# Long convolution and spectral mixing: the second and third transforms on 64x64 quadrants of the array, the filter's spectrum stored once, one tick at a time

## The chip, the core and the metric

The kernel runs on one core of one Trainium2 chip. The metric is the device time of one execution in microseconds (us). A core has a matrix engine (TensorE, PE in the profile; its weight loads are a row of their own, PEld), a vector engine (VectorE, DVE), a scalar engine (ScalarE, ACT), GpSimd (POOL) and SyncE (SP); the last two mostly issue DMAs here. Matmul results land in PSUM, which has eight banks of 512 fp32 columns on 128 partitions; everything else lies in SBUF, also on 128 partitions.

## What is computed

`x` is (8, 5696, 128), `h` is (5696, 128). First a long convolution along the sequence, by FFT of the doubled length; then a spectral layer on its result:

```python
L = 2 * S                                    # S = 5696
y = irfft(rfft(x, L, axis=1) * rfft(h, L, axis=0), L)[:, :S]
X = rfft(y, axis=1)                          # over S
Y[:, :64] = X[:, :64] mixed with w_r, w_i    # complex 128x128 per mode, 64 modes
u = y + irfft(Y, S)
out = u + relu(u @ w_ch)                     # (8, 5696, 128) float32
```

## The kernel before

The transform of length 2S is cut into 64 positions `p` and 89 blocks `q`, which gives `NK` = 90 classes `k` of frequencies. Everything is done by matmul in fp16. Three transforms follow each other.

- **First transform** (`a_tile`, and the loop above it for the filter): over `q`, with the constants in `f1_sb`. The two batches of a pair lie on the two halves of the partitions of `a_sb`, each with its 64 positions.
- **Second transform** (`second` for x, `filter_tick` for h): over the 64 positions, for each class `k`. For batch b the contraction runs over the 64 partitions of that batch, and the result has 128 partitions: 64 real parts over 64 imaginary parts. So a matmul has 64 rows and 128 columns of weights (from `m_sb`) and 128 moving columns. Two of them (real and imaginary input) add up in one PSUM region; batch 0 and batch 1 use the two halves of the rows and two banks.
- **Product** (`products`): spectrum of x times spectrum of h. Since the real part needs Xr·Hr and Xi·Hi on different partitions, the kernel holds the filter twice in `h_sb`: as it is, and with its halves swapped by DMAs (`Hs<-Hs`). VectorE makes both products in one instruction of 2048 elements per partition into `u_s`.
- **Third transform** (`third`): back from 64 frequencies to 64 positions, with two constant 128x128 weights `W1` and `W2` for the two products: for each batch two matmuls of 512 columns into one bank. ScalarE copies the bank to `z_s` (call it Z), a DMA on SP writes `z_s` to a scratch tensor in DRAM.
- **Modes** (`modes_of`): the 64 modes of the second layer, summed straight from `z_s` with the constants `g_sb` into bank 7, eight matmuls of 128 rows by 128 columns per tick.

A **tick** is four classes. A group is a pair of batches; there are four groups, and each has 23 ticks (`NT`; the last has two classes). The order of the work is written out by hand in `tick` and kept by every engine's own queue; `Recorder` only puts in the semaphore waits that the data need. For tick t: the second transform of t, its product, the third transform of t−2 (`LC`), the modes of t−3 (`LM`). Before the change odd ticks are twins: after the product of an odd tick t the second transform of t+1 follows at once, so that the second transforms come in blocks of two ticks (32 matmuls).

PSUM in this stage: two slots of two banks for the second transform (`XSLOT`, banks 0 to 3), three banks that rotate for the third (`ZBANK`, 4, 5, 6), bank 7 for the modes. In three of four ticks ScalarE first copies the spectrum from its slot to SBUF (`copied`, into one of two buffers `x_s`), and VectorE multiplies from there; in the fourth (`straight`, t mod 4 = 3) VectorE reads PSUM itself and holds the slot for as long.

Between the ticks of two groups lies the first transform of the next pair (32 `a_tile`, with the last two third transforms of the group among the first of them). Before the first group lies the filter's transform: 32 `a_tile` of group 0 with the 23 `filter_tick` among them. After the last group the transform back over `q`, the mixing, the residual and the output follow (from about 255 us on); the change doesn't touch them.

The two places that the prediction leans on, besides the diff:

```python
    LC, LM = 2, 3
    XSLOT = [0, 2]
    ZBANK = [4, 5, 6]
...
            zb = [turns("z", ZBANK) for b in range(2)]
```

Of the kernel before, what the change touches and what calls it, by code (L numbers as in the profile page):

```python
# [4 lines left out]
P = 128  # L5
# [118 lines left out]
def bass_long_conv_fft__then__afno_spectral_mix_kernel(nc, x, h, moe_w_r, moe_w_i, moe_w_ch, out):  # L124
# [66 lines left out]
    c_f1 = const("cF1", f1)  # L191
    c_w = const("cW", np.concatenate([w1, w2, np.eye(P)], axis=1))
    c_s4 = const("cS4", s4t)
# [30 lines left out]
    a_h = take(2 * HW * 2)  # L224
    h_sb = at("Hs", 2 * HW, F16, a_h)
    a_g = take(HW * 2)
# [28 lines left out]
    ZP = ZB * 2 * D  # L255
    a_h2, a_xt = a_h + HW * 2, a_x + 4 * S + 2 * B * P
    a_as1, a_m2 = a_as + 2 * S, a_m + 4 * S
# [34 lines left out]
    R = Recorder(nc)  # L292
    for name, n in (("c", 16), ("x", 26), ("z", 8), ("w", 16), ("t", 10), ("s", 8), ("o", 12), ("p", 16), ("q", 10)):
        R.ring(name, n)
# [98 lines left out]

    W1, W2, WI = wc_sb[:, 0:P], wc_sb[:, P:2 * P], wi_sb[:, :]
    XSLOT = [0, 2]
# [58 lines left out]

    HEND = [1, 5, 11, 17, NT - 1]

    def filter_tick(t, banks, eng):
        n = len(ticks[t])
        hb = banks
        for i, k in enumerate(ticks[t]):  # L460
            for r in range(2):
                for dh in range(2):
                    mm(pv(hb[dh], i * DH, [[1, DH]]),
                       ap(m_sb, MW, J * dh, J, k * 3 * J + (J if r == 0 else 0) + dh * J, [[1, P]]),
                       ap(ah_sb, HW, J * dh, J, (2 * k + r) * DH, [[1, DH]]), r == 0, r == 1,
                       AHT + mtok(k) + [("ag", k)], [bank(hb[dh])])
        lo, hi = KT * t * D, (KT * t + n) * D
        old = once("xr", [t_ for r_ in XR for t_ in r_]) if t == 0 else []
        evac(h_sb[:, lo:hi], pv(hb[0], 0, [[DH, n], [512, 2], [1, DH]]), [bank(hb[0]), bank(hb[1])], [("h", t, 0)],
             eng=eng, after=old)  # L470
        if t in HEND:
            g0 = ([-1] + HEND)[HEND.index(t)] + 1
            lo = KT * g0 * D
            for p0, p1 in ((0, J), (J, 0)):
                dma("sync", h_sb[p0:p0 + J, HW + lo:HW + hi], h_sb[p1:p1 + J, lo:hi], "s", [("h", i, 0) for i in range(g0, t + 1)],
                    [("h", i, 1, p0) for i in range(g0, t + 1)])

# [9 lines left out]

    H_ALL = [("h", t, 0) for t in range(NT)] + [("h", t, 1, p0) for t in range(NT) for p0 in (0, J)]
    U_ALL = [("u", i) for i in range(NU)] + [("xs", i) for i in range(NXS)] + \
# [60 lines left out]

    onchip = {}

    def copied(g_, t, sl):
        n = len(ticks[t])
        e = onchip[(g_, t)] = turns("e", list(range(NXS)))
        evac(bass.AP(x_s[e], 0, [[1024, P], [512, 2], [1, n * D]]), pv(sl, 0, [[512, 2], [1, n * D]]), [bank(sl), bank(sl + 1)],
             [("xs", e)], eng="scalar")
        return e

    def twin(g_, t):  # L560
        return t % 2 == 1

# [3 lines left out]
    def slot_of(g_, t):  # L566
        if t == 0:
            return XSLOT[0]
        return XSLOT[((t - 1) // 4 + t) % 2]

    def second(g_, t):
        sl = slot_of(g_, t)
        for i, k in enumerate(ticks[t]):
            for r in range(2):
                for b in range(2):
                    col = k * 3 * J + (J if r == 0 else 0) + b * J
                    mm(pv(sl + b, i * D, [[1, D]]),
                       ap(m_sb, MW, J * b, J, col, [[1, P]]),
                       ap(a_sb, AW, J * b, J, (2 * k + r) * D, [[1, D]]), r == 0, r == 1,
                       AST + mtok(k), [bank(sl + b)])  # L580

    def products(g_, t, sl):
        n = len(ticks[t])
        bk = [bank(sl), bank(sl + 1)]
        i = t % NU
        hv = bass.AP(h_sb, KT * t * D, [[2 * HW, P], [HW, 2], [0, 2], [1, n * D]])
        uv = bass.AP(u_s[i], 0, [[2048, P], [1024, 2], [512, 2], [1, n * D]])
        src = pv(sl, 0, [[0, 2], [512, 2], [1, n * D]])
        if t == 0:
            e = turns("e", list(range(NXS)))  # L590
            evac(bass.AP(x_s[e], 512, [[1024, P], [1, n * D]]), pv(sl + 1, 0, [[1, n * D]]), [bank(sl + 1)], [("xs", e)], eng="scalar")
            hv = bass.AP(h_sb, 0, [[2 * HW, P], [HW, 2], [1, n * D]])
            for b, s_, tok, done in ((0, pv(sl, 0, [[0, 2], [1, n * D]]), bank(sl), ("u", i)),
                                     (1, bass.AP(x_s[e], 512, [[1024, P], [0, 2], [1, n * D]]), ("xs", e), ("u0", i))):
                R.add("vector", lambda e, b=b, s_=s_: e.tensor_tensor(bass.AP(u_s[i], b * 512, [[2048, P], [1024, 2], [1, n * D]]), s_, hv, MULT),  # L595
                      [tok, ("h", t, 0), ("h", t, 1, 0), ("h", t, 1, J)], [done])
            return
        if not straight(g_, t):
            e = onchip.get((g_, t))
            if e is None:  # L600
                e = copied(g_, t, sl)
            src, bk = bass.AP(x_s[e], 0, [[1024, P], [0, 2], [512, 2], [1, n * D]]), [("xs", e)]
        R.add("vector", lambda e: e.tensor_tensor(uv, src, hv, MULT),  # L603
              bk + [("h", t, 0), ("h", t, 1, 0), ("h", t, 1, J)], [("u", i)])

# [9 lines left out]
    def third(g_, s_):  # L615
        if 0 <= s_ < NT:
            n = len(ticks[s_])
            i, zi = s_ % NU, zroom(g_, s_)
            zb = [turns("z", ZBANK) for b in range(2)]
            for b in range(2):  # L620
                for r in range(2):
                    mm(pv(zb[b], 0, [[1, n * D]]), (W1, W2)[r], u_s[i][:, r * 1024 + b * 512:r * 1024 + b * 512 + n * D],
                       r == 0, r == 1, [("u", i), ("wc",)] + ([("u0", i)] if s_ == 0 and b else []), [bank(zb[b])])
                evac(bass.AP(z_s[zi], b * D, [[1024, P], [2 * D, n], [1, D]]),
                     pv(zb[b], 0, [[D, n], [1, D]]), [bank(zb[b])], [("zs", zi, b)], eng="scalar",
                     after=once(("zx", zi, b), Z_OLD) if zi >= NZ else ())
            zo = (g_ * NK + KT * s_) * P * 256
            dma("sync", bass.AP(zs, zo, [[256, P], [P * 256, n], [1, 256]]),
                bass.AP(z_s[zi], 0, [[1024, P], [256, n], [1, 256]]), "z",
                [("zs", zi, 0), ("zs", zi, 1)], [("zd", g_, s_)])  # L630

    def modes_of(g_, s_):
        if 0 <= s_ < NT:
            zi = zroom(g_, s_)
            for b in range(2):
                for i, k in sorted(enumerate(ticks[s_]), key=lambda q: (s_ > 0 or q[1] != 1, q)):
                    if k % 2:
                        o, off, n, sl = pv(MB, b * P, [[1, P]]), (k + 1) // 2 * P, P, (k + 1) // 2
# [5 lines left out]
                    mm(o, z_s[zi][:, i * 256 + b * P:i * 256 + b * P + P], g_sb[:, off:off + n],  # L644
                       k == 1 and b == 0, k == NK - 1 and b == 1, [("g", sl // GP), ("zs", zi, b)], [bank(MB)])
# [255 lines left out]
```

## Time and profile before

| | us |
|---|---|
| median of three runs (380.42 to 383.9) | 381.24 |
| the profiled execution's own time | 385.21 |
| its span, first to last instruction | 383.1 |
| PE busy | 362.8 |
| DVE busy | 305.9 |
| ACT busy | 303.7 |
| filter and first transform of group 0 | 28.3 to 51.1 |
| ticks of the four groups begin at | 51.1, 105.6, 160.0, 214.4 |
| the last block of the modes begins; the back transform starts | 254.3; 255.7 |

The profile is of one execution, on one core, whose mean granted TensorE clock was 0.985. "Busy" of PE is the time in which at least one matmul was under way; matmuls overlap, and one of 128 moving columns is shown as some 217 ns long although the next may start 56 ns after it. So occupancy is better read from start to start: when a block of matmuls begins, and when the next block does. The helper that issues matmuls is line 320, copies are line 308 (ACT) and 312 (DVE), scaled copies 310 and 314; groups are told apart by the tiles behind them: `ps<-As,M` is the second transform of x, `ps<-Ah,M` that of the filter, `ps<-U,Wc` the third, `ps<-G,Zs` (or `Zt`) the modes, `ps<-F,Xin` the first transform; `Xs<-ps` is the copy of the spectrum, `U<-Xs,Hs` the product from SBUF and `U<-ps,Hs` that from PSUM, `Zs<-ps` (or `Zt<-ps`) the evacuation of the third transform.

### The profile page before, as it was taken

How to read it: one execution, taken by the hardware profiler on the slowest of the kernel's cores; microseconds unless marked ns; L12 is line 12 of the kernel's file. 1: busy time of each engine (PE TensorE's matmuls, PEld its weight loads, DVE VectorE, ACT ScalarE, POOL GpSimd, SP SyncE). 2: the span in 40 equal slices, each digit the busy share in tenths (PEclk: the TensorE clock that was granted, in tenths of full speed). 3: DMA queues.
4: the chain of work that ended last, by engine and by line, in shares of the span. 5: the costliest groups of instructions: out<-in, count | busy, mean ns of one | idle time of the engine just before them, and what ended most of it. 6: DMA issues, size and time to landing. Idle time of an engine off the chain costs nothing.

```text
span 383.1 us, 12483 instructions
## 1 busy us (share of the span) xinstructions
PE 362.8 (95%) x5372; PEld 283.6 (74%) x5372; DVE 305.9 (80%) x334; ACT 303.7 (79%) x497; POOL 81.5 (21%) x133
## 2 busy tenths in 40 slices
PE   7999989999989999899999899999979999999994
PEld 7988766667856667766668666668868988988873
DVE  6968898998989998889989887854327767777876
ACT  1358889998989998899998899993447676677785
POOL 8400002320832312723303011339000000000000
PEclk9999999999999999999999999996989999999999
DMA  7999689997999996999997199999999999999768
GB/s 147 194 279 346 151 217 224 282 269 231 116 128 250 231 274 147 145 161 242 241 268 104 15 319 360 339 336 382 407 380 373 361 413 412 412 404 372 303 267 351
DMA packets 83985, 103.94 MB, mean 271 GB/s; under 512 B 22062, under 2 KB 68910, under 8 KB 80450
## 3 DMA queue, kind: packets, MB, share of 16 engines
q1 hardware_dynamic: 59643, 67.73, 51.2%
q0 software_dynamic: 24288, 35.43, 44.0%
q8 instruction: 42, 0.69, 0.7%
q14 instruction: 12, 0.10, 0.1%
HBM read 70.61 MB, written 51.12 MB: 318 GB/s over the span
## 4 chain that ended last, share of the span: by engine, by line
PE 65%; DMA 12%; ACT 10%; DVE 5%; POOL 5%; issue 2%; POOLq 0%; DVEq 0%
PE ps L320 65%; ACT As L310 6%; DMA Xr<-in_x_dram 5%; DMA ZT4b<-zscr 4%; DMA zscr<-Zt 3%; DVE As L314 2%; POOL Xr L317 2%; DVE U L595 1%; ACT R L835 1%; ACT UT L308 1%; ACT Zs L308 1%; DVE O L836 1%; POOL ZT1b L508 0%; POOL ZT3b L508 0%; POOLq L105 0%
## 5 line engine op out<-in xcount | busy, mean ns | idle before, releaser
L320 PE MATMUL ps<-U,Wc 128*128 128x512 f16 (+1 forms) x368 | 94.5, 376 | 0.0
L603 DVE TENSOR_TENSOR U<-Xs,Hs 128x2048 f16<-128x2048 f16 (+1 forms) x68 | 80.5, 1187 | 10.7 <-ACT Xs L308 9.6
L308 ACT CAST Xs<-ps 128x1024 f16<-128x1024 f32 (+1 forms) x72 | 69.5, 971 | 7.0 <-PE ps L320 4.8
L836 DVE TENSOR_TENSOR O<-ps,R 128x512 f32<-128x512 f32 x81 | 52.5, 685 | 21.4 <-ACT R L835 13.9
L308 ACT CAST Zs<-ps 128x512 f16<-128x512 f32 (+1 forms) x126 | 66.1, 605 | 0.0
L835 ACT ACTIVATE R<-ps 128x512 f32<-128x512 f32 x96 | 50.9, 573 | 17.7 <-PE ps L320 17.2
L314 DVE TENSOR_SCALAR As<-ps 128x720 f16<-128x720 f32 x64 | 53.6, 880 | 7.7 <-PE ps L320 6.2
L310 ACT ACTIVATE As<-ps 128x720 f16<-128x720 f32 (+1 forms) x68 | 48.9, 771 | 10.4 <-PE ps L320 9.4
L320 PE MATMUL ps<-F,Xin 128*128 128x180 f16 x512 | 53.7, 250 | 3.4 <-DVE Xin L356 0.9
L320 PEld LDWEIGHTS ps<-F,Xin 128*128 128x128 f16 x512 | 45.3, 155 | 10.7 <-DVE As L314 3.1
L320 PE MATMUL ps<-WI,UT 128*128 128x256 f16 x360 | 52.6, 282 | 0.5 <-DVE O L836 0.4
L320 PE MATMUL ps<-As,M 64*128 64x128 f16 x1440 | 48.6, 217 | 4.5 <-DVE U L595 3.5
L320 PEld LDWEIGHTS ps<-U,Wc 128*128 128x128 f16 x368 | 28.2, 97 | 28.8 <-ACT Zs L308 6.8
L320 PEld LDWEIGHTS ps<-As,M 64*128 64x128 f16 x1440 | 40.3, 94 | 10.3 <-DVE U L595 4.1
L317 POOL DMA_DIRECT2D Xt<-in_x_dram x48 | 25.0, 524 | 102.2 <-PE ps L320 101.6
L603 DVE TENSOR_TENSOR U<-ps,Hs 128x2048 f16<-128x2048 f32 x20 | 45.7, 2283 | 0.0
L308 ACT CAST UT<-ps 128x712 f16<-128x712 f32 x40 | 30.0, 752 | 19.2 <-PE ps L320 18.4
L320 PEld LDWEIGHTS ps<-WI,UT 128*128 128x128 f16 x360 | 39.6, 152 | 4.5 <-issue 1.9
L320 PE MATMUL ps<-IBs,C 128*128 128x356 f16 x128 | 40.5, 326 | 0.7
L320 PEld LDWEIGHTS ps<-G,Zs 128*128 128x128 f16 x492 | 27.0, 96 | 12.7 <-DMA G<-cG 0.3
L308 ACT CAST Zt<-ps 128x512 f16<-128x512 f32 (+1 forms) x58 | 30.9, 602 | 0.4 <-DMA zscr<-Zt 0.4
L312 DVE CAST UT<-ps 128x712 f16<-128x712 f32 x24 | 21.3, 890 | 11.7 <-PE ps L320 11.7
(87 smaller groups left out, 513.0 us busy)
## 6 DMA issues: line engine op xcount, KB each, us to landing
out_dram<-O SPq DMA_DIRECT2D x39, 512.0 KB, 8.6
zscr<-Zs SPq DMA_DIRECT2D x60, 256.0 KB, 7.2
Xt<-in_x_dram POOLq DMA_DIRECT2D x24, 320.0 KB, 6.6
zscr<-Zt SPq DMA_DIRECT2D x28, 256.0 KB, 7.0
W<-wscr POOLq DMA_DIRECT2D x4, 1024.0 KB, 8.7
M<-cM POOLq DMA_DIRECT2D x5, 720.0 KB, 20.8
ZT0a<-zscr SPq DMA_DIRECT2D x3, 1024.0 KB, 13.1
Xr<-in_x_dram POOLq DMA_DIRECT2D x8, 320.0 KB, 14.3
```

What stands on the lines that cost most here:

```text
L308: R.add(e, lambda h_: h_.copy(dst, src), reads, writes, after=after)
L310: R.add(e, lambda h_: h_.activation(dst, src, COPY, scale=scale), reads, writes, after=after)
L312: R.add(e, lambda h_: h_.tensor_copy(dst, src), reads, writes, after=after)
L314: R.add(e, lambda h_: h_.tensor_scalar_mul(dst, src, scale), reads, writes, after=after)
L317: R.add(eng, lambda h_: h_.dma_start(dst, src), reads, writes, ring=ring, after=after)
L320: R.add("tensor", lambda h_: h_.matmul(o, l, r, start=st, stop=sp), reads, writes)
L595: R.add("vector", lambda e, b=b, s_=s_: e.tensor_tensor(bass.AP(u_s[i], b * 512, [[2048, P], [1024, 2], [1, n * D]]), s_, hv, MULT), [tok, ...
L603: R.add("vector", lambda e: e.tensor_tensor(uv, src, hv, MULT), bk + [("h", t, 0), ("h", t, 1, 0), ("h", t, 1, J)], [("u", i)])
L835: R.add("scalar", lambda e: e.activation(rv, src_r, RELU), bk, [("r", i % NR)], after=once(("r", i % NR), G_ALL + XTT + [("y", 0), ("y", 1 ...
L836: R.add("vector", lambda e: e.tensor_tensor(ov, src_u, rv, ADD), bk + [("r", i % NR)], [key + (h_,)], after=once(key, old))
```

## The change

- **Second transform.** A matmul now makes either the real or the imaginary part: 64 rows by 64 columns of weights, 128 moving columns. The 64 result partitions are the lower ones for even classes and the upper ones for odd classes; real and imaginary parts lie side by side in the free dimension (`HB` = 256 columns apart). Four matmuls in a row (`QUADS`) go to the four quadrants of the array: (batch, class parity) = (0,0), (1,1), (0,1), (1,0). A tick has 32 of them where it had 16. `filter_tick` is changed in the same way, and the filter then serves both products from one copy: the DMAs that swapped its halves are gone.
- **Product.** The same number of elements (2048 per partition); the access patterns follow the new layout.
- **Third transform.** The rows are now class parity and frequency, so the contraction is over 64 partitions too: 16 matmuls of 64x64 weights with 512 moving columns (both batches) where there were four of 128x128. The four terms (`at_`) run in the outer loop, the quadrants in the inner one; the two banks of a tick belong to the two class parities, and both are evacuated after the last of the 16 matmuls.
- **Order.** No twins: each tick has its second transform, its product, and the third transform of t−2. The slots of the second transform simply alternate. The modes come for four ticks at once, after the third transform, at t = 6, 10, 14, 18 and 22 (32 matmuls of 128x128); the last three ticks' modes come at the group's end as before.

```diff
-    w1 = np.block([[c, s], [-c, -s]])
-    w2 = np.block([[-s, c], [-s, c]])
+    wj = np.concatenate([c, s, -c, -s], axis=1)
...
+    HB = KT // 2 * D
+    HL = 2 * HB * NT
+    h_sb = at("Hs", HL, F16, a_h)
...
+    QUADS = ((0, 0), (1, 1), (0, 1), (1, 0))
+    MOFF = ((J, 0), (2 * J, J))
...
     def filter_tick(t, banks, eng):
...
+        n2 = len(ticks[t]) // 2
+        for i in range(n2):
+            for ri in range(2):
+                for r in range(2):
+                    for dh, c_ in QUADS:
+                        k = KT * t + 2 * i + c_
+                        mm(pv(banks[dh], (2 * ri + i) * DH, [[1, DH]], J * c_, J),
...
-        if t in HEND:
...
-                dma("sync", h_sb[p0:p0 + J, HW + lo:HW + hi], h_sb[p1:p1 + J, lo:hi], "s", [("h", i, 0) for i in range(g0, t + 1)],
...
     def slot_of(g_, t):
-        if t == 0:
-            return XSLOT[0]
-        return XSLOT[((t - 1) // 4 + t) % 2]
+        return XSLOT[t % 2]
 
     def second(g_, t):
         sl = slot_of(g_, t)
-        for i, k in enumerate(ticks[t]):
-            for r in range(2):
-                for b in range(2):
-                    col = k * 3 * J + (J if r == 0 else 0) + b * J
-                    mm(pv(sl + b, i * D, [[1, D]]),
-                       ap(m_sb, MW, J * b, J, col, [[1, P]]),
...
+        for i in range(len(ticks[t]) // 2):
+            for ri in range(2):
+                for r in range(2):
+                    for b, c_ in QUADS:
+                        k = KT * t + 2 * i + c_
+                        mm(pv(sl + b, ri * HB + i * D, [[1, D]], J * c_, J),
+                           ap(m_sb, MW, J * b, J, k * 3 * J + MOFF[ri][r] + b * J, [[1, J]]),
...
     def products(g_, t, sl):
...
+        hv = bass.AP(h_sb, 2 * HB * t, [[HL, P], [HB, 2], [0, 4], [1, n]])
+        uv = bass.AP(u_s[i], 0, [[2048, P], [1024, 2], [HB, 4], [1, n]])
+        src = pv(sl, 0, [[0, 2], [HB, 4], [1, n]])
...
     def third(g_, s_):
...
-            zb = [turns("z", ZBANK) for b in range(2)]
-            for b in range(2):
-                for r in range(2):
-                    mm(pv(zb[b], 0, [[1, n * D]]), (W1, W2)[r], u_s[i][:, r * 1024 + b * 512:r * 1024 + b * 512 + n * D],
...
+            zb = [turns("z", ZBANK) for c_ in range(2)]
+            for at_, (off, w_) in enumerate(((0, (0, 1)), (HB, (3, 0)), (1024, (3, 0)), (1024 + HB, (2, 3)))):
+                for c_, rz in QUADS:
+                    mm(pv(zb[c_], 0, [[1, 2 * n2 * D]], J * rz, J), ap(wc_sb, 2 * P, J * c_, J, w_[rz] * J, [[1, J]]),
+                       ap(u_s[i], 2048, J * c_, J, off, [[512, 2], [1, n2 * D]]),
...
+            for c_ in range(2):
+                evac(bass.AP(z_s[zi], 2 * D * c_, [[1024, P], [D, 2], [4 * D, n2], [1, D]]),
+                     pv(zb[c_], 0, [[n2 * D, 2], [D, n2], [1, D]]), [bank(zb[c_])], [("zs", zi, c_)], eng="scalar",
...
     def tick(g_, t):
...
-            of_two = t > 0 and twin(g_, t - 1)
-            if not of_two:
-                second(g_, t)
+            second(g_, t)
             products(g_, t, slot_of(g_, t))
-            if twin(g_, t):
-                second(g_, t + 1)
-                if straight(g_, t):
-                    copied(g_, t + 1, slot_of(g_, t + 1))
...
         third(g_, t - LC)
-        modes_of(g_, t - LM)
+        if t % 4 == 2 and t >= 6 and t < NT:
+            for s_ in range(t - 6, t - 2):
+                modes_of(g_, s_)
+        if t >= NT:
+            modes_of(g_, t - LM)
```

More of the change, by code (lines that the diff above doesn't have):

```diff
@@ L292, in bass_long_conv_fft__then__afno_spectral_mix_kernel @@
     R = Recorder(nc)
-    for name, n in (("c", 16), ("x", 26), ("z", 8), ("w", 16), ("t", 10), ("s", 8), ("o", 12), ("p", 16), ("q", 10)):
+    for name, n in (("c", 16), ("x", 26), ("z", 8), ("w", 16), ("t", 10), ("o", 12), ("p", 16), ("q", 10)):
         R.ring(name, n)
@@ L392, in mtok @@
         return t
-    W1, W2, WI = wc_sb[:, 0:P], wc_sb[:, P:2 * P], wi_sb[:, :]
+    WI = wi_sb[:, :]
+    QUADS = ((0, 0), (1, 1), (0, 1), (1, 0))
+    MOFF = ((J, 0), (2 * J, J))
     XSLOT = [0, 2]
@@ L452, in a_tile @@
              [bank(t), bank(t + 1)], [("as", j)], 1.0 / 64, eng=eng, after=once(("hp", j), HP))
-    HEND = [1, 5, 11, 17, NT - 1]
     def filter_tick(t, banks, eng):
-        n = len(ticks[t])
-        hb = banks
-        for i, k in enumerate(ticks[t]):
-            for r in range(2):
[L462 to L467, printed above, removed]
+        n2 = len(ticks[t]) // 2
[5 more added lines that the diff above has]
+                        mm(pv(banks[dh], (2 * ri + i) * DH, [[1, DH]], J * c_, J),
+                           ap(m_sb, MW, J * dh, J, k * 3 * J + MOFF[ri][r] + dh * J, [[1, J]]),
+                           ap(ah_sb, HW, J * dh, J, (2 * k + r) * DH, [[1, DH]]), r == 0, r == 1,
+                           AHT + mtok(k) + [("ag", k)], [bank(banks[dh])])
         old = once("xr", [t_ for r_ in XR for t_ in r_]) if t == 0 else []
-        evac(h_sb[:, lo:hi], pv(hb[0], 0, [[DH, n], [512, 2], [1, DH]]), [bank(hb[0]), bank(hb[1])], [("h", t, 0)],
+        step = D if n2 == 2 else HB
+        evac(bass.AP(h_sb, 2 * HB * t, [[HL, P], [DH, 2], [step, 2 * n2], [1, DH]]),
+             pv(banks[0], 0, [[512, 2], [DH * 2 // n2, 2 * n2], [1, DH]]), [bank(banks[0]), bank(banks[1])], [("h", t, 0)],
              eng=eng, after=old)
-        if t in HEND:
-            g0 = ([-1] + HEND)[HEND.index(t)] + 1
-            lo = KT * g0 * D
-            for p0, p1 in ((0, J), (J, 0)):
-                dma("sync", h_sb[p0:p0 + J, HW + lo:HW + hi], h_sb[p1:p1 + J, lo:hi], "s", [("h", i, 0) for i in range(g0, t + 1)],
-                    [("h", i, 1, p0) for i in range(g0, t + 1)])
     def load_g(i):
@@ L486, in load_w @@
             "p", WD, [("w", i)] + (XIN if i == 0 else []), after=pace)
-    H_ALL = [("h", t, 0) for t in range(NT)] + [("h", t, 1, p0) for t in range(NT) for p0 in (0, J)]
+    H_ALL = [("h", t, 0) for t in range(NT)]
     U_ALL = [("u", i) for i in range(NU)] + [("xs", i) for i in range(NXS)] + \
@@ L549, in bass_long_conv_fft__then__afno_spectral_mix_kernel @@
     XBANKS = [bank(0), bank(1), bank(2), bank(3)]
-    onchip = {}
     def copied(g_, t, sl):
-        n = len(ticks[t])
-        e = onchip[(g_, t)] = turns("e", list(range(NXS)))
-        evac(bass.AP(x_s[e], 0, [[1024, P], [512, 2], [1, n * D]]), pv(sl, 0, [[512, 2], [1, n * D]]), [bank(sl), bank(sl + 1)],
+        n2 = len(ticks[t]) // 2
+        e = turns("e", list(range(NXS)))
+        evac(bass.AP(x_s[e], 0, [[1024, P], [HB, 4], [1, n2 * D]]), pv(sl, 0, [[HB, 4], [1, n2 * D]]), [bank(sl), bank(sl + 1)],
              [("xs", e)], eng="scalar")
         return e
-    def twin(g_, t):
-        return t % 2 == 1
     def straight(g_, t):
@@ L566, in slot_of @@
     def slot_of(g_, t):
-        if t == 0:
-            return XSLOT[0]
-        return XSLOT[((t - 1) // 4 + t) % 2]
+        return XSLOT[t % 2]
     def second(g_, t):
         sl = slot_of(g_, t)
-        for i, k in enumerate(ticks[t]):
-            for r in range(2):
-                for b in range(2):
-                    col = k * 3 * J + (J if r == 0 else 0) + b * J
-                    mm(pv(sl + b, i * D, [[1, D]]),
-                       ap(m_sb, MW, J * b, J, col, [[1, P]]),
-                       ap(a_sb, AW, J * b, J, (2 * k + r) * D, [[1, D]]), r == 0, r == 1,
-                       AST + mtok(k), [bank(sl + b)])
+        for i in range(len(ticks[t]) // 2):
[5 more added lines that the diff above has]
+                           ap(m_sb, MW, J * b, J, k * 3 * J + MOFF[ri][r] + b * J, [[1, J]]),
+                           ap(a_sb, AW, J * b, J, (2 * k + r) * D, [[1, D]]), r == 0, r == 1,
+                           AST + mtok(k), [bank(sl + b)])
@@ L582, in products @@
     def products(g_, t, sl):
-        n = len(ticks[t])
+        n = len(ticks[t]) // 2 * D
         bk = [bank(sl), bank(sl + 1)]
         i = t % NU
-        hv = bass.AP(h_sb, KT * t * D, [[2 * HW, P], [HW, 2], [0, 2], [1, n * D]])
-        uv = bass.AP(u_s[i], 0, [[2048, P], [1024, 2], [512, 2], [1, n * D]])
-        src = pv(sl, 0, [[0, 2], [512, 2], [1, n * D]])
         if t == 0:
             e = turns("e", list(range(NXS)))
[L591 to L596, printed above, removed]
+            evac(bass.AP(x_s[e], 512, [[1024, P], [1, 512]]), pv(sl + 1, 0, [[1, 512]]), [bank(sl + 1)], [("xs", e)], eng="scalar")
+            hv = bass.AP(h_sb, 0, [[HL, P], [HB, 2], [0, 2], [1, n]])
+            for b, s_, tok, done in ((0, pv(sl, 0, [[0, 2], [HB, 2], [1, n]]), bank(sl), ("u", i)),
+                                     (1, bass.AP(x_s[e], 512, [[1024, P], [0, 2], [HB, 2], [1, n]]), ("xs", e), ("u0", i))):
+                R.add("vector", lambda e, b=b, s_=s_: e.tensor_tensor(bass.AP(u_s[i], b * 512, [[2048, P], [1024, 2], [HB, 2], [1, n]]), s_, hv, MULT),
+                      [tok, ("h", t, 0)], [done])
@@ L597, in products @@
             return
+        hv = bass.AP(h_sb, 2 * HB * t, [[HL, P], [HB, 2], [0, 4], [1, n]])
+        uv = bass.AP(u_s[i], 0, [[2048, P], [1024, 2], [HB, 4], [1, n]])
+        src = pv(sl, 0, [[0, 2], [HB, 4], [1, n]])
         if not straight(g_, t):
[L599 to L604, printed above, removed]
+            e = copied(g_, t, sl)
+            src, bk = bass.AP(x_s[e], 0, [[1024, P], [0, 2], [HB, 4], [1, n]]), [("xs", e)]
@@ L606, in bass_long_conv_fft__then__afno_spectral_mix_kernel @@
+        R.add("vector", lambda e: e.tensor_tensor(uv, src, hv, MULT), bk + [("h", t, 0)], [("u", i)])
     Z_OLD = [("ag", k) for k in range(NS, NS + 8 * (NZX - NZ))]
@@ L617, in third @@
             n = len(ticks[s_])
+            n2 = n // 2
             i, zi = s_ % NU, zroom(g_, s_)
-            zb = [turns("z", ZBANK) for b in range(2)]
-            for b in range(2):
-                for r in range(2):
-                    mm(pv(zb[b], 0, [[1, n * D]]), (W1, W2)[r], u_s[i][:, r * 1024 + b * 512:r * 1024 + b * 512 + n * D],
[L623 to L626, printed above, removed]
+            zb = [turns("z", ZBANK) for c_ in range(2)]
[3 more added lines that the diff above has]
+                       ap(u_s[i], 2048, J * c_, J, off, [[512, 2], [1, n2 * D]]),
+                       at_ == 0, at_ == 3, [("u", i), ("wc",)] + ([("u0", i)] if s_ == 0 else []), [bank(zb[c_])])
+            for c_ in range(2):
+                evac(bass.AP(z_s[zi], 2 * D * c_, [[1024, P], [D, 2], [4 * D, n2], [1, D]]),
+                     pv(zb[c_], 0, [[n2 * D, 2], [D, n2], [1, D]]), [bank(zb[c_])], [("zs", zi, c_)], eng="scalar",
+                     after=once(("zx", zi, c_), Z_OLD) if zi >= NZ else ())
             zo = (g_ * NK + KT * s_) * P * 256
@@ L644, in modes_of @@
                     mm(o, z_s[zi][:, i * 256 + b * P:i * 256 + b * P + P], g_sb[:, off:off + n],
-                       k == 1 and b == 0, k == NK - 1 and b == 1, [("g", sl // GP), ("zs", zi, b)], [bank(MB)])
+                       k == 1 and b == 0, k == NK - 1 and b == 1, [("g", sl // GP), ("zs", zi, k % 2)], [bank(MB)])
     def tick(g_, t):
```

5 lines of the change are left out of this document (2 added, 3 removed).

## The prediction

> **What bounds the kernel now.** First the page: how busy each engine is.
>
> ```profile
> PE 362.8 (95%) x5372; PEld 283.6 (74%) x5372; DVE 305.9 (80%) x334; ACT 303.7 (79%) x497; POOL 81.5 (21%) x133
> ```
>
> The change touches the ticks and the filter's stage, so the second view is busy time by stretch: all ticks of group 0, and then four ticks out of them (us; PE, PEld, DVE, ACT, POOL, granted clock).
>
> ```profile
> 51.10:89.30 38.20, 37.33 (x605) 24.57 (x606) 35.90 (x31) 36.56 (x59) 8.30 (x16) 1.00 1.03 255
> ...
> 58.09:65.09 7.00, 7.00 (x113) 4.63 (x113) 5.72 (x5) 6.89 (x13) 2.07 (x4) 1.00 1.02 208
> ```
>
> PE and ACT are both full. Which one decides, and how closely the other follows, is in the third view, the instructions in order of time over those ticks (start, length).
>
> ```profile
> 58.09 1.07 PE L320 MATMUL ps<-As,M 64*128 64x128 f16 x32
> ...
> 59.09 1.04 PE L320 MATMUL ps<-U,Wc 128*128 128x512 f16 x4
> 59.73 1.07 ACT L308 CAST Zs<-ps 128x512 f16<-128x512 f32 x2
> ...
> 59.96 0.49 PE L320 MATMUL ps<-G,Zs 128*128 128x2 f16 x8
> 60.28 1.02 PE L320 MATMUL ps<-U,Wc 128*128 128x512 f16 x4
> 60.69 1.03 ACT L308 CAST Xs<-ps 128x1024 f16<-128x1024 f32 x1
> ...
> 61.15 0.49 PE L320 MATMUL ps<-G,Zs 128*128 128x2 f16 x8
> ...
> 61.57 1.07 PE L320 MATMUL ps<-As,M 64*128 64x128 f16 x32
> 61.59 1.11 ACT L308 CAST Zs<-ps 128x512 f16<-128x512 f32 x2
> ...
> 62.67 1.01 ACT L308 CAST Xs<-ps 128x1024 f16<-128x1024 f32 x1
> ...
> 63.58 1.08 ACT L308 CAST Zs<-ps 128x512 f16<-128x512 f32 x2
> ...
> 64.23 0.11 PEld L320 LDWEIGHTS ps<-U,Wc 128*128 128x128 f16 x2 [0.36 <-ACT Zs L308]
> ...
> 65.09 1.07 PE L320 MATMUL ps<-As,M 64*128 64x128 f16 x32
> ```
>
> From start to start PE has no hole: two second transforms 1.00, third 0.87, modes 0.33, third 0.86, modes 0.42, next block. Two ticks are 3.48 to 3.53 us, four 7.00: the ticks are bound by PE. Singly, a pair of 64-row matmuls (the two row halves start 3 ns apart) follows the last pair after 56 ns; but from the last one of a block to the first with 128 rows it is 147 ns, and back 149. So each switch of shape costs about 0.092, four times in four ticks. ACT, start to start: a copy of the spectrum 0.90 (62.67 to 63.58), an evacuation 0.477 (a pair 0.96, 59.73 to 60.69), so three copies and eight evacuations are 6.5 of the 7.00. The load at 64.23 waited for an evacuation, because with three banks each tick needs one that the tick before has just filled; it cost 0.044.
>
> **The change, part by part.** I write S, T, M for a tick's second transform, third transform and modes on PE, C for the copy, Z0 and Z1 for the two evacuations.
>
> S: 32 matmuls of 128 columns in eight sets of four quadrants. The trace has none on 64x64. Its nearest row is the pair on two row halves, 56 ns for both; so a set is 56 ns if four run together and 112 if two do: S is 0.448 or 0.896 (before: 0.448). T: four sets of 512 columns, 0.216 each (matmuls of 512 columns start every 215 to 217 ns): 0.863 (as before), or 1.726. I take the four, since the row halves already run side by side at no visible cost, and keep the other end. [...]
>
> M: 0.326 a tick, now four together, 1.30; switches of shape go from four to two per four ticks, as S and T are now of one shape. So PE's own work per four ticks falls from 7.00 to 4×(0.448+0.863)+1.30+0.18 = 6.73. ACT and DVE have the same instructions with the same elements (evacuation: runs of 128 either way; product: 1024 adjoining elements per operand either way): nothing.
>
> What is lost is the overlap, and it is a wait. Before, a tick's first bank was ready after half of T, and ACT evacuated it while PE filled the second. Now both banks are ready only at the end of T. T of the next tick writes the bank of Z0 with its second matmul, and behind that PE's whole queue waits: the rest of T, the next S, later the modes. Hence a loop per tick: last set of T starts 0.647 after the first and is done 0.380 later (length of a 512-column matmul), 0.035 to ACT, Z0 0.605, 0.035 back to PE: 1.70 from T to T, against 0.863+0.448 = 1.31 of PE's work. Three kinds of tick:
>
> - With a copy: ACT's queue is C, Z0, Z1: 0.90+2×0.477 = 1.854, more than the loop. ACT decides.
> - After a tick whose product reads PSUM there is no C; the loop decides: 1.70.
> - With the batch of modes: T 0.863 + switch 0.092 + four M 1.304 + switch 0.092 + S 0.448 = 2.80 from T to T. PE decides, and ACT, whose two evacuations take 1.1, stands idle. The batch always comes just ahead of the straight tick (t = 2 mod 4), which has no C to fill the hole.
>
> Four ticks: 2.80+1.70+2×1.854 = 8.21 against 7.00. In a group from the first T to the 21st (four batches, five ticks by the loop, eleven with copy): 4×2.80+5×1.70+11×1.854 = 40.1; before, 34.5 (53.59 to 88.09). That is +5.6. From the 21st T to the 22nd another batch lies between: 0.863+1.304+0.184 = 2.35 against 1.19, +1.2. Four groups: +27.2; the last ticks of the last group go by the loop, 1.70 against 1.29: +0.4. Together +27.6.
>
> The rest. The two T among the first `a_tile` of the next pair are now another shape: four switches, 0.37 per group; that stage waits for ACT and DVE (108 matmuls in 10.9 us, 101 ns each where 77 are possible), so I charge nothing of at most 1.1. The filter's matmuls (64 columns) run at 28 ns a pair before; in sets of four the same stage time, at two together 0.45 more for each of 11 blocks, +5 at most, in a stage where ACT and DVE are as full (19 of 22.8 us): I take 0. The ten `Hs<-Hs` DMAs on SP's queue go; the first product was released by PE (51.76), not by them: 0. S of the next tick waits for its slot, freed by the copy of two ticks ago or a straight product of 2.28; in the loop above it comes before T is due. Waits of DVE stay shorter than ACT's.
>
> Sum: 385.21 + 27.6 = 412.8 for an execution like the profiled one. That one is 4.0 above the median, which the change doesn't touch, so for the median 381.24 + 27.6 = **409**.
>
> **Rivals.**
>
> *Two quadrants at a time.* S 0.896, T 1.726. Then the loop is 0.863 longer, 2.57, and PE's own 2.62 is as long; the batch tick 4.11: four ticks 3×2.62+4.11 = 12.0, +5.0 over 7.00, about 23 such periods: +110, 491. For it: no matmul with 64 columns beside another in this trace. Against it: the row halves.
>
> *Weight loads one after the other.* The matmuls are four together, but the loads of a set are not. Bound from rows: in the tail of the output a 128x64 load is followed by its matmul after 31 ns (377.663 to 377.694), as a 128x128 one is (296.637 to 296.668); so a load is 31 at most and a set 4×31 = 124, S 0.99, T still hidden by 216. The loop tick becomes 1.86, the copy tick stays, the batch tick 3.35: +0.7 per four ticks, and with the 22nd T +3.5 a group: +14 more, 423. [...]
>
> *PE stays the bound, and the kernel is faster.* Place: every tick, between Z0 and the next T. If PE has the bank back after 1.31 rather than 1.70, only PE's 6.73 counts: −0.27 per four ticks, −6, 375. It decides from 0.39 less in the loop. For it: before, an evacuation held PE up by only 0.044. Against: the evacuation then started at half of T, and ACT's 1.854 in the copy ticks would remain.
>
> *Half of it.* The holes of PE take up most of the batch: an M lying in the 0.39 of each tick would cost nothing, and four ticks would be 3×1.854+1.70 = 7.26: +6 to +10, 389. Against: all four queues are in order, and the batch stands in one place.
>
> [...]
>
> **Chances and numbers.** Loop and batch as reckoned, 400 to 417: 0.57. Loads in line, 423: 0.12. Two at a time, 491: 0.11. Faster, 375: 0.09. Half, 389: 0.08. No change: 0.03. The range 388 to 428 holds 0.77 of it; at its ends stand the half and the loads (423 with the filter's 5). One per cent, 3.8 us, is about what a measurement of this kernel can tell from no change. Faster by more 0.09, within 0.03, slower by more 0.88.
>
> **What will show it.** Right: T starts 1.70, 1.85, 1.85 and 2.80 apart in turn; one unbroken block of 32 mode matmuls every fourth tick with ACT idle for over 1 us beside it; before T's weights waits put down to ACT's evacuation; four ticks of 8.2; S in 0.45. Wrong: S or T much longer than 0.45 and 0.86 from start to start (quadrants or loads in line); no hole on PE (the loop is shorter than I think); an evacuation or product with another mean than 0.61 and 1.22; a lower granted clock in the ticks, if the holes bring that.

## The result and the profile after

The changed kernel takes 442.2 us in the median of four runs (440.66 to 444.51) against 381.36 beside it: 1.159 times the time before, interval 1.151 to 1.167. The forecast was 409, range 388 to 428. The direction and the mechanism named in the prediction are there, but as much again came on top, from something that neither the prediction nor any of its rivals names.

The page of the changed kernel, its busy times and the engines' shares of the chain that ended last:

```profile
PE 384.9 (87%) x8276; PEld 300.5 (68%) x8276; DVE 310.1 (70%) x334; ACT 304.6 (69%) x497; POOL 81.4 (18%) x133
...
PE 58%; ACT 20%; issue 9%; DMA 5%; DVE 4%; POOL 2%; DVEq 0%; ACTq 0%; POOLq 0%
```

ACT and DVE do hardly more work than before (305 against 304, 310 against 306), and PE is busy for 22 us more (385 against 363) of the 59 by which the span grew (442.4 against 383.1), so most of the time is in waits. "issue" is time in which an engine waited for nothing that the profile shows: 9% of 442 us. The same line of the kernel before has 2%:

```profile
PE 65%; DMA 12%; ACT 10%; DVE 5%; POOL 5%; issue 2%; POOLq 0%; DVEq 0%
```

Where the time went by stretch: the ticks of the four groups and the back transform with all that follows it (us; PE, PEld, DVE, ACT, POOL, granted clock, DMA share, GB/s).

```profile
57.50:111.20 53.70, 42.66 (x1233) 28.41 (x1234) 38.09 (x32) 37.59 (x60) 8.33 (x16) 1.00 0.80 175
126.70:180.30 53.60, 43.09 (x1232) 28.45 (x1232) 38.09 (x32) 37.46 (x60) 9.46 (x18) 1.00 0.87 169
195.80:248.70 52.90, 43.09 (x1232) 28.23 (x1232) 38.10 (x32) 37.44 (x60) 9.92 (x19) 1.00 0.89 171
264.10:318.00 53.90, 46.59 (x1268) 30.34 (x1269) 33.39 (x24) 39.15 (x64) 10.58 (x16) 0.97 0.81 249
318.00:442.40 124.40, 115.75 (x1651) 100.94 (x1649) 81.58 (x125) 81.84 (x140) 8.75 (x9) 0.95 0.93 370
```

The ticks of a group take 53 to 54 us where they took 39.1 (the last group 41.3 with its end): +55.4 together. The first tick begins at 57.5, not 51.1: +6.4 in the filter's stage. The first transforms between the groups are 15.3 to 15.6 long (15.2 to 15.4 before), together +0.5, and the end is 3.0 shorter. That adds up to the span's 59.3.

How the ticks look inside, in order of time (start, length; in brackets the idle time before and what ended it):

```profile
69.75 0.30 PEld L321 LDWEIGHTS ps<-As,M 64*64 64x64 f16 x17
69.75 0.42 PE L321 MATMUL ps<-As,M 64*64 64x128 f16 x16
...
71.44 0.42 PE L321 MATMUL ps<-As,M 64*64 64x128 f16 x16 [1.27 <-issue]
...
71.66 1.06 PE L321 MATMUL ps<-U,Wc 64*64 64x512 f16 x16
...
72.52 0.65 PE L321 MATMUL ps<-As,M 64*64 64x128 f16 x32
72.75 1.07 ACT L309 CAST Zs<-ps 128x512 f16<-128x512 f32 x2 [3.06 <-PE ps L321]
...
72.97 1.48 PE L321 MATMUL ps<-U,Wc 64*64 64x512 f16 x16
73.39 0.57 PEld L321 LDWEIGHTS ps<-U,Wc 64*64 64x64 f16 x15 [0.37 <-ACT Zs L309]
...
77.77 0.48 PEld L321 LDWEIGHTS ps<-As,M 64*64 64x64 f16 x32 [1.91 <-issue]
```

Three things are to be seen. An undisturbed second transform takes 0.447 from start to start (72.52 to 72.97) and a third 0.863 (71.66 to 72.52): the four quadrants run at the same time, 56 and 216 ns a set. The third transform at 72.97 stops after its first matmul until an evacuation has freed its second bank: the loop of the prediction. And the second transform at 69.75 stops in its middle, between two matmuls that wait for no semaphore: from 69.95 to 71.44 none starts, 1.5 us. Before the one at 77.77 it is 1.8 us (75.97 to 77.77). In the ticks such holes are new.

I numbered all records of PE in order of start, weight loads, matmuls and the sequencer's semaphore instructions. Every hole of this kind over 0.6 us ends with a record whose number is 193 more than a multiple of 256; from start to start there are 27 over 0.3 us at that place, 38.2 us in all. The page has a queue that may well move just such pieces: all its packets have 16 KB, which for 256 instructions would be 64 bytes each. The queue before and after (packets, MB, share of the 16 DMA engines):

```profile
q8 instruction: 42, 0.69, 0.7%
```

```profile
q8 instruction: 65, 1.06, 0.9%
```

PE had 10,744 matmuls and loads, now 16,552: 23 pieces more, and the queue has 23 packets more. The single packets show when a piece is fetched: in the ticks, where a hole follows, the packet begins 2.0 to 5.3 us after the piece before it began to run (3.5 in the mean), and PE goes on 2.2 to 2.7 us after the packet's start (2.35 in the mean). So these pieces followed one another after 4.8 to 7.7 us, 5.85 in the mean. Before, 256 instructions lasted about 8 us in the ticks (224 took 7.00 us) and no hole over 0.3 us stood at that place; the one of the whole span, 1.07 us at 42.2, lies in the filter's stage. After, with 448 instructions in the prediction's 8.21 us, they would last 4.7. That the next piece is asked for only when the last begins to run was an assumption of mine; the trace shows only when its packet moves.

### The profile page after: what moved, and what is told of

It reads as the page before. It is cut to its first block, busy times and chain, and to the rows that moved or that the text cites. A ratio compares the mean times of both kernels' runs of the same rounds, so it can differ in the third digit from the quotient of the medians.

```text
span 442.4 us, 18314 instructions
## 1 busy us (share of the span) xinstructions
PE 384.9 (87%) x8276; PEld 300.5 (68%) x8276; DVE 310.1 (70%) x334; ACT 304.6 (69%) x497; POOL 81.4 (18%) x133
## 4 chain that ended last, share of the span: by engine, by line
PE 58%; ACT 20%; issue 9%; DMA 5%; DVE 4%; POOL 2%; DVEq 0%; ACTq 0%; POOLq 0%
PE ps L321 58%; ACT As L311 6%; ACT Zs L309 6%; ACT Xs L309 4%; DMA Xr<-in_x_dram 4%; ACT Zt L309 2%; DVE As L315 2%; POOL Xr L318 2%; DVE U L583 1%; ACT R L824 1%; ACT UT L309 1%; DMA zscr<-Zt 1%; DVE UT L313 0%; ACT XT L311 0%; DVE O L825 0%
## 5 line engine op out<-in xcount | busy, mean ns | idle before, releaser
L321 PE MATMUL ps<-U,Wc 64*64 64x512 f16 (+1 forms) x1472 | 118.7, 380 | 16.6 <-issue 8.2
L592 DVE TENSOR_TENSOR U<-Xs,Hs 128x2048 f16<-128x2048 f16 (+1 forms) x68 | 81.1, 1193 | 44.5 <-ACT Xs L309 36.7
L309 ACT CAST Zs<-ps 128x512 f16<-128x512 f32 (+1 forms) x126 | 67.9, 603 | 32.2 <-PE ps L321 32.1
L321 PE MATMUL ps<-As,M 64*64 64x128 f16 x2880 | 65.5, 219 | 22.3 <-issue 17.4
L321 PEld LDWEIGHTS ps<-As,M 64*64 64x64 f16 x2880 | 55.1, 107 | 40.1 <-issue 22.0
L309 ACT CAST Xs<-ps 128x1024 f16<-128x1024 f32 (+1 forms) x72 | 70.9, 991 | 14.0 <-PE ps L321 13.9
L321 PEld LDWEIGHTS ps<-U,Wc 64*64 64x64 f16 x1472 | 42.9, 107 | 49.6 <-ACT Zs L309 14.3
L321 PE MATMUL ps<-F,Xin 128*128 128x180 f16 x512 | 54.6, 254 | 4.0 <-issue 2.2
L321 PE MATMUL ps<-F 128*128 128x180 f16 x260 | 26.0, 256 | 2.5 <-DMA F<-cF 2.5
```

What stands on the lines that cost most here:

```text
L309: R.add(e, lambda h_: h_.copy(dst, src), reads, writes, after=after)
L321: R.add("tensor", lambda h_: h_.matmul(o, l, r, start=st, stop=sp), reads, writes)
```

## The experiments

**Theory A**: PE's instruction stream is fetched in pieces of 256, and the change, which makes 112 instructions per tick of 56, runs into the rate of that; the prediction's loop and batch are there beside it. Against it: the holes come from the quadrants or the new order (B), the loop and batch cost nothing (C), or the batch and loop bound the ticks whatever the holes (D).

### More instructions in the kernel before (b_split)

```diff
+            for hd, r in ((0, 0), (0, 1), (1, 0), (1, 1)):
                 for b in range(2):
-                    mm(pv(sl + b, i * D, [[1, D]]),
+                    mm(pv(sl + b, i * D + hd * DH, [[1, DH]]),
...
+                for c4 in range(4):
+                    for r in range(2):
+                        lo = r * 1024 + b * 512 + c4 * w4
+                        mm(pv(zb[b], c4 * w4, [[1, w4]]), (W1, W2)[r], u_s[i][:, lo:lo + w4],
```

> The kernel before, with the same work cut into more instructions and nothing else: each matmul of the second transform in two of 64 columns, each of the third in four of 128 columns. TensorE's stream then has as many instructions per tick as the changed kernel (112 with the weight loads, 56 before), in the old shapes, order and banks. Theory A (PE's instructions are fetched in pieces of 256, each asked for only when the one before it has begun, and one takes 5 to 6 us in this stage): four ticks hold 448 instructions, so they take 9.0 to 10 us in place of 7.0, holes of about 1 to 3 us stand at every 256th instruction, +50 to +75 us, 430 to 455. Theory B (the holes come from the 64x64 quadrants or from the new order): no holes, only the matmuls' own extra time (128 columns at 56 ns against a quarter of 216: 0.03 per tick), 381 to 386.

Measured: 418.3 against 381.8, ratio 1.100 (1.092 to 1.108). The old shapes get the same holes. In order of time, matmuls of the second transform:

```profile
66.93 0.32 PE L320 MATMUL ps<-As,M 64*128 64x64 f16 x10
69.47 0.96 PE L320 MATMUL ps<-As,M 64*128 64x64 f16 x54 [2.22 <-issue]
```

Ten matmuls of a block of 64, then 2.4 us of nothing, again at record 193 after a multiple of 256 (number 2497). Theory B is out as the cause of the holes: neither quadrant nor new order is needed. The size was overrated: 418.3 lies below the 430 to 455 expected, and a group's ticks took 47 to 51 us, where 9.0 to 10 us per four ticks had meant 52 to 57. A piece took 5.3 us in the mean of the first group here.

### Half as many instructions in the changed kernel (a_wide)

```diff
-        for i in range(len(ticks[t]) // 2):
+        w2 = len(ticks[t]) // 2 * D
+        for i in range(1):
...
-                        mm(pv(sl + b, ri * HB + i * D, [[1, D]], J * c_, J),
+                        mm(pv(sl + b, ri * HB + i * D, [[1, w2]], J * c_, J),
...
-                           ap(a_sb, AW, J * b, J, (2 * k + r) * D, [[1, D]]), r == 0, r == 1,
+                           ap(a_sb, AW, J * b, J, (2 * k + r) * D, [[1, w2]]), r == 0, r == 1,
```

and the same in `filter_tick`.

> The changed kernel with half as many, twice as wide matmuls in the second transform of x and of the filter (256 and 128 moving columns in place of 128 and 64): the second class of each pair is left out, its columns are filled with the first one's weights. TensorE's time for the moving columns is the same, the instructions of four ticks fall from 448 to 320. Theory A (fetching of instructions): the holes at every 256th instruction go, four ticks take the 8.2 us of the prediction's loop and batch, the ticks of a group 46 in place of 53.6, the filter's stage gets its 5 to 6 us back: 442 - 30 - 6 = 402 to 412. Theory B (quadrants or order as such): the holes stay, 435 or more. Theory C (the loop over the banks and the batch cost nothing, all of the loss is fetching): back to 385 or less.

Measured: 411.2 against 381.8, ratio 1.084 (1.077 to 1.090); 31 us less than the changed kernel. The ticks of the first group take 46.6 us (50.1 to 96.7), and the filter's stage ends at 50.1. Holes over 0.3 us at the place of the fetch: four in all, 2.1 us (27 and 38.2 us in the changed kernel). What is left is the prediction's order:

```profile
67.53 1.14 ACT L309 CAST Zt<-ps 128x512 f16<-128x512 f32 x2
...
68.23 0.57 PEld L321 LDWEIGHTS ps<-U,Wc 64*64 64x64 f16 x15 [0.67 <-ACT Zt L309]
...
69.22 0.82 PE L321 MATMUL ps<-G,Zs 128*128 128x2 f16 x16
69.39 1.18 ACT L309 CAST Zt<-ps 128x512 f16<-128x512 f32 x2
...
69.88 0.81 PE L321 MATMUL ps<-G,Zt 128*128 128x2 f16 x16
...
70.62 0.63 PE L321 MATMUL ps<-As,M 64*64 64x256 f16 x16
...
71.08 1.03 PE L321 MATMUL ps<-U,Wc 64*64 64x512 f16 x16
...
72.16 1.07 ACT L309 CAST Zt<-ps 128x512 f16<-128x512 f32 x2 [1.59 <-PE ps L321]
...
72.80 0.57 PEld L321 LDWEIGHTS ps<-U,Wc 64*64 64x64 f16 x15 [0.41 <-ACT Zt L309]
```

32 mode matmuls from 69.22 to 70.6, ScalarE idle for 1.59 us behind them, and the loads of the third transform waiting for `Zt`. Since its first matmul runs ahead here, the ends of the third transforms are the fairer measure: they stand 1.74, 1.89, 1.90 and 2.83 apart, together 8.36 (forecast 1.70, 1.854, 1.854, 2.80; 8.21). So this run separates the two causes: loop and batch are worth the 29 us between 381.8 and 411.2 (theory C is out), the supply of instructions the other 31. The 29 is a net figure: by the profiles the ticks of the four groups took some 30 us more than before, while the filter's stage was 0.7 shorter and the end, from the back transform on, 4.3.

### Modes in every tick, with and without the holes (a_each, a_wide_each)

```diff
-        if t % 4 == 2 and t >= 6 and t < NT:
-            for s_ in range(t - 6, t - 2):
-                modes_of(g_, s_)
-        if t >= NT:
-            modes_of(g_, t - LM)
+        modes_of(g_, t - LM)
```

> The changed kernel with the modes of t-3 in every tick, as before, in place of four ticks' modes at once. The number of instructions is the same. Theory A (fetching bounds the ticks): next to nothing, 435 to 445, since 448 instructions take the same 9 to 10 us however they are ordered. Theory D (the batch and the loop bound the ticks and the holes are beside them): four ticks fall from 8.2 to 7.3 and the end of a group by 1, so -17 to -20, about 424.

Measured: 432.9 (428.6 to 435.0), ratio 1.139 (1.128 to 1.149): 9 less than the changed kernel, between the two expectations but nearer to A. At the place of the fetch there are still 23 holes over 0.3 us that wait for no semaphore, 32.9 us in all.

> Both: half as many, twice as wide matmuls in the second transforms (the second class of each pair left out) and the modes of t-3 in every tick. Theory A with the prediction's loop and batch: without the holes the batch is worth its hole on ScalarE, four ticks 7.3 to 7.5, a group's ticks 41 to 43; 385 to 397, 15 to 20 less than with the wide matmuls alone. If the batch costs nothing: the same as with the wide matmuls alone.

Measured: 397.3, ratio 1.045 (1.036 to 1.053): 14 less than a_wide, just short of the 15 to 20 expected. So the batch of modes costs 14 us when instructions are at hand and 9 when they are not; that the fetch hides part of it was my guess for the difference, which no run shows. Together the two edits bring back 45 of the 61 us. Six holes are left, 4.4 us, 2.1 of it in one hole of the first group, whose ticks took 46.3 us; those of the others took 42.7 to 44.5. There the third transforms end 1.85 apart for most of the time. That is PE's own work: 0.447 + 0.863 + 0.326 for the modes and two switches of shape in every tick, 1.82.

### Loop and batch alone in the kernel before (b_ends, b_batch)

```diff
             zb = [turns("z", ZBANK) for b in range(2)]
-            for b in range(2):
-                for r in range(2):
+            for r in range(2):
+                for b in range(2):
                     mm(pv(zb[b], 0, [[1, n * D]]), (W1, W2)[r], u_s[i][:, r * 1024 + b * 512:r * 1024 + b * 512 + n * D],
                        r == 0, r == 1, [("u", i), ("wc",)] + ([("u0", i)] if s_ == 0 and b else []), [bank(zb[b])])
+            for b in range(2):
                 evac(bass.AP(z_s[zi], b * D, [[1024, P], [2 * D, n], [1, D]]),
...
```

> The kernel before with one edit: in the third transform the two products run in the outer loop and the batches in the inner one, so that both banks are ready only at its end, as in the changed kernel; the same matmuls, the same number of instructions. If the loop third transform, first evacuation, next third transform is what the prediction says (0.65 + 0.38 + 0.04 + 0.605 + 0.04 = 1.70 from one to the next, with the modes now inside it): four ticks go from 7.0 to 7.9, a group's ticks from 39.1 to about 46, +25 to +30 us, 406 to 412. If the loop costs nothing (the other bank is enough of a buffer): 381 to 384.

Measured: 390.5 (386.2 to 394.4), ratio 1.020 (1.013 to 1.026); ticks 41.1 a group, four ticks 7.37. Far less than expected, and the reason is in my reading of the edit. The profile:

```profile
68.54 1.04 PE L320 MATMUL ps<-U,Wc 128*128 128x512 f16 x4
69.40 1.07 ACT L308 CAST Zt<-ps 128x512 f16<-128x512 f32 x2 [0.18 <-PE ps L320]
69.41 0.49 PE L320 MATMUL ps<-G,Zt 128*128 128x2 f16 x8
69.74 1.12 PE L320 MATMUL ps<-U,Wc 128*128 128x512 f16 x4
```

The evacuation begins 0.86 after the third transform, not 1.07: with whole-array matmuls one after the other the first bank is ready one matmul before the end, and the next transform has one matmul to do before it needs that bank. These two times 0.216 make the loop 1.27, hardly more than the 1.20 that lay between two third transforms anyway. In the quadrant form both banks end with the same set and the second bank is wanted by the second matmul, 31 ns after the first where nothing is waited for (71.656 and 71.687 in the changed kernel). So this run doesn't copy the changed kernel's loop; a_wide shows it directly.

```diff
-        modes_of(g_, t - LM)
+        if t % 4 == 2 and t >= 6 and t < NT:
+            for s_ in range(t - 6, t - 2):
+                modes_of(g_, s_)
+        if t >= NT:
+            modes_of(g_, t - LM)
```

> The kernel before with the modes of four ticks at once at t = 6, 10, 14, 18 and 22 and nothing else changed. If the batch starves ScalarE as the prediction says: four ticks go from 7.0 to 7.3 (ScalarE decides in the ticks without modes, TensorE in the one with them), a group's ticks from 39.1 to about 42.5 with the batch at its end, +12 to +16 us, 393 to 398. If only the switches of shape matter (two fewer in four ticks): -4, 377.

Measured: 388.1, ratio 1.017 (1.013 to 1.021), below the 393 to 398 expected. Four ticks take 7.37, near the 7.3, but a group's ticks 41.1 where 42.5 was expected: the 0.37 per four ticks alone makes 2.1 us a group, all of the 2.0 that came on top, so the batch at a group's end cost nothing that can be seen. Two switches of shape fewer in four ticks did not make it faster. In both runs the end, from the back transform on, was about 4 us shorter than before, as it was by 3 in the changed kernel. No run was made for its cause, but the traces show a part: before, PE waits there 2.6 us for reads of the scratch tensor (2.1 for `ZT4b<-zscr`), and in these three runs it waits for none.

### What the fetch waits for (a_quiet)

```diff
+            if g_ < 2:
+                return
             dma("sync", bass.AP(zs, zo, [[256, P], [P * 256, n], [1, 256]]),
...
-                bass.AP(zs, (g_ * 2 * NK + r0) * J * 256 + c_ * ZB * 256, [[J * 256, n], [1, ZP]]),
+                bass.AP(zs, (max(g_, 2) * 2 * NK + r0) * J * 256 + c_ * ZB * 256, [[J * 256, n], [1, ZP]]),
```

> The changed kernel without the writes of the third transform's result to DRAM in the first two groups (that part is left out; the back transform reads the third group's result in their place). In these two groups 90 per cent of the DMA packets of the ticks are gone; in the other two nothing is changed. If the fetch of TensorE's instructions takes as long as it does because it stands behind other DMAs: the pieces of 256 instructions come faster in groups 0 and 1, their ticks fall from 53.6 towards the 46 of the loop and batch, those of groups 2 and 3 stay at 53 to 54. If the fetch has its own fixed time: all four groups stay at 53 to 54.

Measured: 428.8 against 381.9, ratio 1.124 (1.118 to 1.130). The ticks of the four groups (columns as above):

```profile
57.30:103.90 46.60, 42.55 (x1232) 27.56 (x1232) 38.09 (x32) 37.06 (x60) 8.30 (x16) 1.00 0.43 66
119.50:166.10 46.60, 42.55 (x1232) 27.59 (x1232) 38.09 (x32) 37.07 (x60) 9.39 (x18) 1.00 0.57 80
181.60:233.90 52.30, 44.35 (x1233) 29.59 (x1233) 38.10 (x32) 37.35 (x60) 9.93 (x19) 0.97 0.88 172
249.20:301.90 52.70, 45.38 (x1268) 29.55 (x1269) 33.40 (x24) 38.97 (x64) 10.58 (x16) 1.00 0.82 254
```

The same number of matmuls, the same order; without the writes 46.6, to the tenth what a_wide needed, and no hole over 0.3 us; with them 52.3 and 52.7. In the ticks of the first two groups the packets of the instruction queue began 0.7 us in the mean after the piece before, over all pieces, where in the changed kernel they began 2.4 us after it; the packet itself was no shorter (1.1 against 1.0 us). So the fetch is late because of the kernel's own DMAs, some 10,700 small packets in a group's ticks here, and it loses its time before its packet starts. Where it waits the trace doesn't show.

### Fewer instructions with the whole computation (a_trow)

```diff
...
-                for c_, rz in QUADS:
-                    mm(pv(zb[c_], 0, [[1, 2 * n2 * D]], J * rz, J), ap(wc_sb, 2 * P, J * c_, J, w_[rz] * J, [[1, J]]),
+                for c_ in range(2):
+                    mm(pv(zb[c_], 0, [[1, 2 * n2 * D]]), ap(wc_sb, 2 * P, J * c_, J, w_ * J, [[1, P]]),
```

> The changed kernel with the third transform in 8 matmuls of 64 rows by 128 columns in place of 16 of 64 by 64: the two column halves of a quadrant pair in one instruction, the same streaming time, 16 instructions fewer per tick (384 in four ticks in place of 448), and a switch of shape between second and third transform that costs about 0.09 each way. If the supply of instructions bounds the ticks: -4 to -5 us a group in spite of the switches, 420 to 428. If not: the switches add up to 0.18 a tick, 442 to 455.

Measured: 422.3 (418.1 to 425.6), ratio 1.098 (1.093 to 1.103): 20 less than the changed kernel for an edit that adds two switches of shape per tick, and within the 420 to 428 of theory A. In its profiled execution, of 425.6 us, the ticks took 48.7 to 51.2 a group, and 15 holes over 0.3 us summed to 17.2 us.

No version with quadrants came under the kernel before. At the 5.3 us a piece of b_split, my estimate for the changed kernel's 448 instructions in four ticks is 9.3 us, where the kernel before needs 7.0; and without the holes loop and batch still take 8.4 (a_wide).

## Why the prediction was wrong, step by step

- **Quadrants.** Right: S 0.447 and T 0.863 against 0.448 and 0.863. "Two at a time" and "loads in line" did not happen: the four loads of a set start within 10 ns after a hole (71.438 to 71.448), and within 38 in a running stream (71.873 to 71.911). In line a set would have taken up to 124 ns by that rival's bound; the sets stand 56 ns apart. A load of 64 rows and 64 columns is shown as 107 ns long, where those of 128 columns in the ticks before were 94 to 97.
- **The loop and the batch.** Right, in size too: 1.74, 1.89, 1.90, 2.83 against 1.70, 1.854, 1.854, 2.80 where nothing else disturbs; +7.5 us a group in a_wide against 6.8 forecast, and some 30 us in all ticks against 27.6. The changed kernel's own matmuls stand the same way in a_quiet's first two groups (1.73, 1.89, 1.90, 2.84). So "half of it", modes that hide in the loop's hole, did not happen either.
- **"The filter's matmuls ... I take 0"**, bounded at +5. Wrong: the stage took 6.4 us more. Its four largest holes are 2.5, 1.3, 0.6 and 1.5 us, and the granted clock over it was 0.88. The quadrants are not the reason: a_wide, in quadrants too but with half the instructions, had 1.00 and 22.1 us (22.8 before).
- **The term that was missing.** The step that failed is "PE's own work per four ticks falls from 7.00 to 6.73": it counted columns and switches, and gave no price to an instruction as such, though the change adds 5,808 of them. No rival did either. In its place the runs showed holes a multiple of 256 instructions apart, worth 31 us (442.2 against a_wide's 411.2), about as much as loop and batch. The kernel before showed where to look: its one hole without a wait, 1.07 us at 42.2 (shown as 0.8 for "issue"), lies in the stage whose pieces of 256 lasted 5 to 6 us, and the page counts the fetches. From the rows of before I could have had a rough estimate, though from one hole: a piece 5 to 6 us, four ticks 448/256 of it, 8.8 to 10.5 us, above the 8.2 of loop and batch; together some 430 to 460.
- **The back transform, "the change doesn't touch them".** It became 3.0 us shorter, and the sum has no term for it. Less waiting for the scratch tensor's reads is the part that the traces show.
- **The rival on the other side** ("PE stays the bound") needed a loop shorter by 0.39. It was not: 1.73 to 1.74 against the 1.70 forecast. What the removed `Hs<-Hs` DMAs bring was not tested by itself; the filter's stage of a_wide leaves at most 0.7 us for it.

## What to carry to other kernels

Count instructions as a resource of its own: before a matmul is cut into smaller ones, compare how long 256 of the engine's instructions last in that stage with how long a fetch takes under the stage's DMA load (here 4.7 us against 4.8 to 7.7). Holes without a wait, an equal number of instructions apart in an engine's stream, were its mark here: 27 over 0.3 us, all a multiple of 256 apart. Fewer, wider instructions left 2.1 us of their 38.2 (a_wide), and without the small writes none was left in two groups' ticks (a_quiet). And when a matmul is spread over quadrants, look at when its banks become ready: here results that used to come one after the other came all at once, and the evacuation that was hidden turned into a loop of 1.73 to 1.74 us against 1.31 of PE's own work.

## What was not expected of the hardware

- PE's instructions come by DMA in pieces of 16 KB, beside the kernel's data: 23 such packets more for 5,808 matmuls and loads more. In the ticks, where a hole followed, a packet of that queue began 2.0 to 5.3 us after the piece before had begun, and without the kernel's small writes the holes were gone (52.3 and 52.7 us a group with them, 46.6 without, in one run).
- The granted clock fell after two of the long holes, and not after others. From the filter's stage to the end of the changed kernel's ticks the granted clock is 0.50 twice, from 38.1 to 45.0 us and from 290.7 to 294.1, each time within 2 us of the end of a long hole (2.5 us at 33.9, 3.1 us at 286.3); after other holes of over 2 us, at 92.5 and 144.6, it stays at 1.00. So the holes are not shown to be the cause, and the kernel before has 0.50 too, from 258.8 to 265.6 us, with no hole of this kind before it but the one at 42.2.
- Four 64x64 quadrants, each with its own weights and moving data, run with no loss: 56 ns a set of 128 columns, as two 64-row halves before, and 216 a set of 512, as one 128x128 matmul.
